# Pair 0's setup, query loads and phi moved in the opening of an attention kernel followed by two MLP layers, with weight decoding from step 6 and the first layer item in any step

## The chip, the cores and the metric

One core of a Trainium2 chip runs the whole kernel. The metric is device time in microseconds (us) of one execution; the kernel before took 1056.87 us (median of 3 runs, 1056.28 to 1060.51).

## What is computed

The reference is causal attention with a memory branch, and two dense layers behind it. B, H, S, D are 4, 8, 576, 64.

```
scores = (q @ k^T) / 8, causal mask;  a = softmax(scores);  local = a @ v
phi(x) = where(x > 0, x, exp(x) - 1) + 1
mem    = (phi(q) @ M_prev) / (phi(q) . z_prev + 1e-6)
x      = g * mem + (1 - g) * local          g = sigmoid(beta), one per head
h = x @ w_in;  x = (h - tanh(h)) @ w_out            # layer 1, 2304 x 512 x 2048
h = x @ w2_in; x = (P(h) / Q(h)) @ w2_out           # layer 2, a cubic over a quadratic
```

## The kernel before

Attention works on pairs of heads: 16 pairs, 0 to 15. A pair has five units, four blocks of 128 query rows and one with the 64 last rows of both heads. The loop runs over steps `s`: unit `u` has its scores in step `u`, so pair `n` begins in step `5n`. In one step the stages follow a fixed list, `ORDER`, and each stage works on an older unit (`LAGS`): scores of the newest unit (TensorE, line 414) with the eviction from PSUM, mask and row minimum (VectorE, line 423); `numer`, the exponentials (ScalarE, line 436) and reciprocal sums (VectorE, lines 441 and 444) one step later; `scale` (GpSimd, line 450) two steps later; `transposes` (TensorE, ScalarE copies) three; `values`, the products `pv` and `pw`, four; `leave`, the copy into `x` (VectorE, line 787), five.

The memory branch needs phi of the queries for each pair. `prep` lists its pieces with the step, relative to the pair's first, in which each is issued: `phi1` (a minimum on VectorE, line 347), `phi2` (an exponential on ScalarE, line 351), `phi3` (VectorE, line 355), `norm1` (GpSimd, line 361, result `pz`), `norm2` (VectorE, from line 370), `norm3` (GpSimd, line 378), and the TensorE transposes `php` (line 388). `late` alters these steps for pair 0. Before the first step `start` issues the key loads, `setup` (the query loads, mask, identity, constants), pair 0's other loads, `setup2` (the gate g and 1 - g, called gg and omg, lines 832 to 839) and pair 0's `phi1`.

All loads go through SyncE's queue (SP). Every engine takes its instructions in program order, so an instruction that waits holds up those behind it on its engine.

Two streams run beside attention. `Background` (`bg`) loads the weights of layer 1, which come as 64-bit words, and decodes them: per half chunk an absolute value (ScalarE, line 164), a clamp, a pair of shifts and two merges (VectorE, lines 166 to 174, tile `wf`), and for the first four chunks a rounding copy (ScalarE) and a remainder (GpSimd, line 186). From step `BG_FROM` on `tick` advances it each step, and starts a half chunk in steps with `s % 5` in `START_A`, (2, 4); from step 34 on only at 2. The other stream is layer 1 itself: when four pairs have left, `fill` calls `advance`. It first prepares the inputs of a tile (`xs`: a rounding copy on ScalarE, a remainder on GpSimd, line 595), and then starts *items*: an item is a *head*, 12 matmuls `h` (line 603), and three steps later a *tail*, 12 matmuls `y` (line 650). Items start in steps with `s % 5` in `ITEM_AT`, (2, 4), the first at step 27. An item waits until its weight chunk is decoded.

Of the kernel before, what the change touches and what calls it, by code (L numbers as in the profile page):

```python
# [18 lines left out]
P = 128  # L19
# [5 lines left out]
ITEM_AT = (2, 4)  # L25
START_A, START_B, MIX_FROM = (2, 4), (2,), 34

BG_FROM = 10
AGE_A, AGE_B, AGE_C = 1, 3, 4

LESS_AT = 4
# [29 lines left out]
def kernel(  # L61
# [21 lines left out]
    nc = tc.nc  # L83
    B, NP, _, _, S = qd.shape
    H, D = 2 * NP, mz.shape[2] // 2
# [4 lines left out]
    TAIL = S - NQ * P  # L90
    TB = NQ * P
# [120 lines left out]
    class Background:  # L212
# [36 lines left out]
        def tick(self, start=True):  # L249
            self.now += 1  # L250
            for item in list(self.live):
                item[0] += 1
                self.held -= item[0] == item[1]
                if next(item[3], self) is self:
                    self.live.remove(item)
            if (
                start and self.ns < self.nl
                and self.now >= self.loaded[self.ns] + self.q[self.ns][4]
                and len(self.live) < len(self.ring["wf"])
            ):  # L260
                _, done, key, work, _ = self.q[self.ns]
                self.ns += 1
                next(work)
                self.live.append([1, done, key, work])
            while self.nl < len(self.q) and self.held < len(self.ring["wraw"]):
                load, _, key, *_ = self.q[self.nl]
                load(*key)
                self.held += 1
                self.loaded.append(self.now)
                self.nl += 1  # L270
# [21 lines left out]
    class Attention:  # L292
# [24 lines left out]
        def load_q(self, n, _=None):  # L317


            n += 1  # L320
            if n < len(self.pair):
                t = self.pair[n]["rq"] = self.cp["rq"][n % 2]
                src = qd[n // NP, n % NP]
                nc.sync.dma_start(t[0:D, P:P + TB], src[0:D, 0, 0:TB])
                nc.sync.dma_start(t[D:P, TAIL:P + TB], src[D:P, 1])
                nc.sync.dma_start(t[0:D, 0:TAIL], src[0:D, 0, TB:S])

        def load_k(self, n, _=None):
# [205 lines left out]

        def late(self, m, f, r):

            if m == 0:
                return r + (f in (self.phi3, self.norm1, self.norm2, self.norm3))
            return r

        def start(self, setup, setup2):

            self.load_k(-1)
            setup()
            self.load_n(0)
            setup2()
            self.phi1(0, None)

        def step(self, s, fill, tick):
            n, i = divmod(s, self.NU)  # L550
            m, at = divmod(s - LAG_T - PHI_AT, self.NU)
            for o in ORDER:
                if o in LAGS:
                    u = self.unit(s - LAGS[o])
                    if u:
                        getattr(self, o)(*u)
                elif o == "fill":
                    fill()
                elif o == "tick":
                    tick()  # L560
                elif o == "phiT":
                    if at == 0 and 0 <= m < len(self.pair):
                        self.phiT(m)
                elif o == "loads":
                    if i == 0 and n < len(self.pair):
                        self.load_n(n + 1)
                        self.load_v(n)
                elif o == "prep":
                    for r, f, arg in self.prep:
                        for m_ in range(len(self.pair)):  # L570
                            if m_ * self.NU + self.late(m_, f, r) == s:
                                f(m_, arg)
# [234 lines left out]
    ]  # L807

    def setup():
        for t in cp["rq"]:  # L810
            nc.vector.memset(t[0:D, TAIL:P], 0.0)
            nc.vector.memset(t[D:P, 0:TAIL], 0.0)
        attn.load_q(-1)
        nc.sync.dma_start(cp["g"], beta.partition_broadcast(P))
        nc.gpsimd.memset(cp["mask"], 0.0)
        nc.gpsimd.affine_select(
            out=cp["mask"][:, TB:TB + P], in_=cp["mask"][:, TB:TB + P],
            compare_op=ALU.is_ge, fill=NEG, base=0, pattern=[[-1, P]],
            channel_multiplier=1,
        )  # L820
        make_identity(nc, cp["ident"])
        for e in range(2):
            r = slice(e * TAIL, (e + 1) * TAIL)
            nc.vector.tensor_copy(cp["mask4"][r], cp["mask"][0:TAIL, TB:TB + TAIL])
        for sm in cp["sm"]:
            nc.vector.memset(sm, 1e-9)
        for pz in cp["pz"]:
            nc.vector.memset(pz[:, :, :, D:D + 1], 1e-6)

    def setup2():  # L830
        g, omg = cp["g"], cp["omg"]
        nc.scalar.activation(g, g, AF.Exp, scale=-1.0)
        nc.vector.tensor_scalar(g, g, 1.0, None, ALU.add)
        nc.vector.reciprocal(g, g)
        nc.vector.tensor_scalar(omg, g, -1.0, 1.0, ALU.mult, ALU.add)
        o2 = omg.rearrange("r (p e) -> r p e", e=2)
        for e in range(2):
            r = slice(e * TAIL, (e + 1) * TAIL)
            nc.vector.tensor_copy(cp["omg4"][r], o2[r, :, e])
# [3 lines left out]
    attn = Attention(x_put, cp, sp, bS, bT, bV)  # L843
    xs_a = Split(x_of, TA, [(wka, f"xs{k}", 1) for k in range(NK)], nc.gpsimd)
    one = Moe1(xs_a, range(NT // TA), TA, FA, wka, bHa, bYa, False, nc.vector)
    flow = {"n": 0, "line": [None, None, None]}

    def advance(start, eager=False):

        line = flow["line"]  # L850
        one.leave()
        if line[0]:
            one.gate1(*line[0])
        if line[1]:
            one.gate2(*line[1])
        if line[2]:
            one.tail(*line[2])
        new = None
        if flow["n"] < len(one.items):
            t, f = one.items[flow["n"]]  # L860
            if (t + 1) * TA <= attn.done * S:
                if t not in xs_a.of and not eager:
                    xs_a.ready(t)
                elif start and (eager or bg.has(1, f)):
                    new = (t, f)
                    one.head(t, f)
                    flow["n"] += 1
                    if eager and f == FA[-1] and (t + 2) * TA <= NT:
                        xs_a.ready(t + 1)
        flow["line"] = [new] + line[:2]  # L870
        return new is not None
# [5 lines left out]
    for f in FB[len(FB) - KEEP:]:  # L877
        bg.add(1, f, w_keep)
    attn.start(setup, setup2)
    mixed = False  # L880

    def fill():
        advance(s % attn.NU in ITEM_AT and s < len(attn.units) - attn.NU)

    for s in range(attn.nsteps):
        if attn.done and not mixed:
# [3 lines left out]
        def tick():  # L890
            if s >= BG_FROM:
                bg.tick(s % attn.NU in (START_A if s < MIX_FROM else START_B))
# [59 lines left out]
    for s in range(ni + 2):  # L952
        if s < ni:
            t, f = items[s]
# [110 lines left out]
```

## Time and profile before

| | |
|---|---|
| profiled execution | 1056.03 us, of which the span from first to last instruction is 1054.2 us |
| runs | median 1056.87 us of 3, 1056.28 to 1060.51 |
| TensorE busy | 1026.5 us (97%) |
| VectorE, ScalarE, GpSimd busy | 785.2, 700.5, 383.5 us |
| granted TensorE clock, mean | 0.996 |

The time of the execution beside its span leaves 1.83 us for what lies outside the first and last instruction. TensorE busy counts matmuls from start to modelled end, so a busy TensorE can still be slower than its peak. In the rows further down PE is TensorE, PEld its weight loads, DVE VectorE, ACT ScalarE, POOL GpSimd, and SPq the issue of a DMA on SyncE's queue.

### The profile page before, as it was taken

What the parts mean: (1) busy time and instruction counts of PE and PEld (TensorE: products, weight loads), DVE (VectorE), ACT (ScalarE), POOL (GpSimd) and SP (SyncE); (2) the same over time, 40 slices, a digit from 0 to 9 for tenths busy, and PEclk for the clock granted to TensorE, in tenths of its full rate; (3) what the DMA queues carried; (4) which work ended last, traced back from release to release, by engine and by line L of the source; (5) the groups of instructions that cost most, each with busy time, mean ns of one, the idle gap of its engine ahead of it and who ended that gap; (6) DMA issues with size and microseconds to landing.
All of it is one profiled execution on the core that took longest, in us unless ns stands there. A gap on an engine that the chain in (4) does not pass through costs nothing.

```text
span 1054.2 us, 18289 instructions
## 1 busy us (share of the span) xinstructions
PE 1026.5 (97%) x6544; PEld 901.8 (86%) x6544; DVE 785.2 (74%) x1737; ACT 700.5 (66%) x1508; POOL 383.5 (36%) x391
## 2 busy tenths in 40 slices
PE   6989999999999999999999998989999999999998
PEld 4657777777699999999999998979999999999997
DVE  5898766766678766767576666998787787877875
ACT  5777775776655543333333456889888888888886
POOL 5788665664534210101010103662332422323221
PEclk9999999999999999999999999999999999999999
DMA  5445343252142334444444331100000000000000
GB/s 154 156 127 164 103 136 110 82 163 82 54 141 80 121 95 136 120 120 122 126 140 123 120 121 61 41 1 30 1 1 31 2 30 1 1 31 1 21 11 30
DMA packets 35147, 84.03 MB, mean 80 GB/s; under 512 B 5872, under 2 KB 7920, under 8 KB 35056
## 3 DMA queue, kind: packets, MB, share of 16 engines
q1 hardware_dynamic: 35056, 82.86, 25.8%
q8 instruction: 51, 0.84, 0.3%
q14 instruction: 40, 0.33, 0.1%
HBM read 66.59 MB, written 16.25 MB: 79 GB/s over the span
## 4 chain that ended last, share of the span: by engine, by line
PE 84%; DVE 9%; ACT 3%; issue 2%; POOL 1%; DMA 1%; SPq 0%; ACTq 0%; POOLq 0%; DVEq 0%
PE h L603 33%; PE y L650 17%; PE y L733 17%; PE s L414 5%; PE tp L466 4%; PE pv L500 4%; PE pw L514 1%; PE pv L488 1%; DVE vA L699 1%; DVE vA L709 1%; PE php L388 1%; DVE gl L639 1%; POOL pz L361 1%; DVE wf L171 1%; DVE vG L711 1%
## 5 line engine op out<-in xcount | busy, mean ns | idle before, releaser
L603 PE MATMUL h<-xs,w 128*128 128x384 f32 (+1 forms) x2448 | 438.2, 327 | 6.2 <-DVE g L715 2.7
L603 PEld LDWEIGHTS h<-xs,w 128*128 128x128 f32 x2448 | 408.5, 188 | 17.0 <-POOL xs L595 3.4
L650 PE MATMUL y<-gh,w 128*128 128x384 f32 (+1 forms) x864 | 216.1, 318 | 0.2 <-ACT gh L638 0.2
L733 PE MATMUL y<-w,gh 128*128 128x512 f32 x576 | 179.7, 393 | 0.0
L650 PEld LDWEIGHTS y<-gh,w 128*128 128x128 f32 x864 | 151.5, 188 | 1.3 <-ACT gh L638 0.6
L450 POOL TENSOR_SCALAR p<-p,sm,omg 128x128 f32<-128x128 f32 (+2 forms) x144 | 116.1, 816 | 74.9 <-ACT p L436 25.2
L650 PE MATMUL y<-gl,w 128*128 128x384 f32 (+1 forms) x432 | 136.9, 317 | 1.2 <-DVE gl L639 0.9
L595 POOL TENSOR_TENSOR xs<-x,xs 128x256 fp32r<-128x256 f32 (+1 forms) x56 | 49.1, 901 | 231.4 <-ACT xs L594 216.1
L632 ACT ACTIVATE g<-h 128x384 f32<-128x384 f32 (+1 forms) x108 | 49.4, 458 | 118.6 <-PE h L603 117.7
L733 PEld LDWEIGHTS y<-w,gh 128*128 128x128 f32 x576 | 107.0, 188 | 17.4
L633 DVE TENSOR_TENSOR g<-h,g 128x384 f32<-128x384 f32 (+1 forms) x108 | 55.0, 509 | 86.2 <-ACT g L632 85.9
L733 PE MATMUL y<-w,gl 128*128 128x512 f32 x288 | 114.1, 396 | 1.1 <-POOL gl L722 1.0
L722 POOL TENSOR_TENSOR gl<-g,gh 128x384 fp32r<-128x384 f32 x48 | 50.6, 1055 | 153.2 <-ACT gh L720 141.4
L470 ACT COPY pT<-tp 128x512 f32<-128x512 f32 (+2 forms) x112 | 55.8, 529 | 60.9 <-PE tp L466 59.1
L722 POOL TENSOR_TENSOR gl<-vG,gh 128x384 fp32r<-128x384 f32 x47 | 51.3, 1092 | 115.1 <-ACT gh L720 112.0
L638 ACT CAST gh<-g 128x384 fp32r<-128x384 f32 (+1 forms) x108 | 51.8, 480 | 58.2 <-PE y L650 55.8
L436 ACT ACTIVATE p<-p,sm 128x128 f32<-128x128 f32 (+2 forms) x144 | 83.8, 591 | 9.3 <-DVE sm L441 4.8
L709 DVE TENSOR_TENSOR vA<-vA,vC 128x384 f32<-128x384 f32 x96 | 57.8, 602 | 41.1 <-ACT vC L703 41.1
L423 DVE CUSTOM_DVE_ANT_0 p<-s,mask 128x512 f32<-128x512 f32 (+4 forms) x160 | 70.3, 476 | 22.2 <-PE s L414 22.0
L414 PE MATMUL s<-rk,rq 64*128 64x128 f32 (+5 forms) x320 | 77.0, 496 | 6.7 <-DMA rq<-in_qd_dram 4.9
L650 PEld LDWEIGHTS y<-gl,w 128*128 128x128 f32 x432 | 81.2, 188 | 2.0 <-DVE gl L639 2.0
L639 DVE TENSOR_TENSOR gl<-g,gh 128x384 fp32r<-128x384 f32 (+1 forms) x108 | 60.7, 562 | 27.7 <-ACT gh L638 27.6
(91 smaller groups left out, 1619.2 us busy)
## 6 DMA issues: line engine op xcount, KB each, us to landing
wraw<-in_w_in_dram SPq DMA_DIRECT2D x32, 512.0 KB, 4.1
wraw<-in_w_out_dram SPq DMA_DIRECT2D x32, 512.0 KB, 4.0
wk<-wf SPq DMA_DIRECT2D x44, 256.0 KB, 4.4
wx<-wk SPq DMA_DIRECT2D x22, 512.0 KB, 3.2
qn<-in_qn_dram SPq DMA_DIRECT2D x16, 320.0 KB, 3.9
vn<-in_vn_dram SPq DMA_DIRECT2D x16, 320.0 KB, 5.3
rk<-in_kd_dram SPq DMA_DIRECT2D x32, 144.0 KB, 5.3
out_dram<-o SPq DMA_DIRECT2D x18, 256.0 KB, 2.0
```

What stands on the lines that cost most here:

```text
L414: nc.tensor.matmul(ps[c][:, 0:k1 - k0], d["rq"][r, c0:c0 + P], d["rk"][r, k0:k1], start=True, stop=True,)
L423: nc.vector.tensor_tensor_reduce(out=pts[-1][:, k0:k1], in0=ps[c][:, 0:k1 - k0], in1=mask, scale=-0.125, scalar=3.0e38, op0=ALU.add, op1=A ...
L436: nc.scalar.activation(pt, pt, AF.Exp, bias=sm[:, 4 + e:5 + e], scale=-1.0, accum_out=sm[:, 2 * e:2 * e + 1],)
L450: nc.gpsimd.tensor_scalar(pt, pt, v["sm"][:, 6 + e:7 + e], og[:, c:c + 1], ALU.mult, ALU.mult)
L470: nc.scalar.copy(t[:, 0:w, :].rearrange("r t c -> r (t c)"), ps[:, 0:w * P])
L603: nc.tensor.matmul(ps[:, 0:T], wi_of(layer, f, wp, k), xs[k][:, xp], start=(n == 0), stop=(n == 3 * NK - 1),)
L633: nc.vector.tensor_tensor(v["g"], v["h"], v["g"], ALU.subtract)
L639: self.lo.tensor_tensor(v["gl"], v["g"], v["gh"].bitcast(F32), ALU.subtract)
L650: nc.tensor.matmul(ps, wo_of(1, f, w)[:, m * P:(m + 1) * P], v[g], start=(first and j == 0 and m % n == 0), stop=(last and j == 2), skip_g ...
L709: nc.vector.tensor_tensor(n["A"], n["A"], n["C"], ALU.mult)
L722: eng.tensor_tensor(o["gl"], o["G"], o["gh"].bitcast(F32), ALU.subtract)
L733: nc.tensor.matmul(acc_of[t][m], g[:, c], wo_of(2, f, w), start=(first and j == 0), stop=(last and j == 2),)
```

## The change

In the opening, two of the three query loads of pair 0 are issued on ScalarE's queue, and ahead of the memsets. `setup2` and pair 0's `phi1` and `phi2` are issued in step 1, behind the scores and exponentials of that step, in place of before step 0 and in step 0. The decoder starts at step 6 in place of step 10. Until the first item has started, an item may start in any step.

```diff
-BG_FROM = 10
+BG_FROM = 6
...
-                nc.sync.dma_start(t[0:D, P:P + TB], src[0:D, 0, 0:TB])
-                nc.sync.dma_start(t[D:P, TAIL:P + TB], src[D:P, 1])
+                eng = nc.sync if n else nc.scalar
+                eng.dma_start(t[0:D, P:P + TB], src[0:D, 0, 0:TB])
+                eng.dma_start(t[D:P, TAIL:P + TB], src[D:P, 1])
                 nc.sync.dma_start(t[0:D, 0:TAIL], src[0:D, 0, TB:S])
...
-            if m == 0:
-                return r + (f in (self.phi3, self.norm1, self.norm2, self.norm3))
+            if m == 0 and f not in (self.load_k, self.load_q):
+                return max(1, r + 1)
             return r
...
             self.load_n(0)
-            setup2()
-            self.phi1(0, None)
+            self.setup2 = setup2
...
                 elif o == "prep":
+                    if s == 1:
+                        self.setup2()
...
     def setup():
+        attn.load_q(-1)
         for t in cp["rq"]:
             nc.vector.memset(t[0:D, TAIL:P], 0.0)
             nc.vector.memset(t[D:P, 0:TAIL], 0.0)
-        attn.load_q(-1)
...
     def fill():
-        advance(s % attn.NU in ITEM_AT and s < len(attn.units) - attn.NU)
+        starts = s % attn.NU in ITEM_AT or not flow["n"]
+        advance(starts and s < len(attn.units) - attn.NU)
```

ScalarE's first instructions before, from the start of the program (`p_0_0` is the exponential of head 0 in unit 0; ISA rows further down are the evictions of line 423):

```order
L832 ACT_TABLE_LOAD
L832 ACTIVATE gg<-gg 128x8
L351 ACTIVATE phi_143<-phi_143 128x640
L436 ACTIVATE p_0_0_155,sm_98<-p_0_0_155,sm_98 128x128
L436 ACTIVATE p_0_1_157,sm_98<-p_0_1_157,sm_98 128x128
L436 ACTIVATE p_1_0_170,sm_99<-p_1_0_170,sm_99 128x256
```

The same place on ScalarE after the change:

```order
L325 DMA rq_102<-in_qd_dram 64x512
L326 DMA rq_102<-in_qd_dram 64x576
L437 ACT_TABLE_LOAD
L437 ACTIVATE p_0_0_147,sm_98<-p_0_0_147,sm_98 128x128
L437 ACTIVATE p_0_1_149,sm_98<-p_0_1_149,sm_98 128x128
L834 ACTIVATE gg<-gg 128x8
L352 ACTIVATE phi_175<-phi_175 128x640
L437 ACTIVATE p_1_0_161,sm_99<-p_1_0_161,sm_99 128x256
```

The gate and phi have moved from ahead of unit 0's exponentials to between those of unit 0 and of unit 1. On VectorE, after the change, the same five small instructions of the gate and the minimum of phi stand behind the evictions of units 0 and 1 and the sums of unit 0:

```order
L424 ISA p_1_1_163,sm_99<-s_1_1_158,mask 128x256
L424 ISA sm_99 128x1
L442 TENSOR_REDUCE sm_98<-sm_98 128x2
L445 RECIPROCAL sm_98<-sm_98 128x2
L835 TENSOR_SCALAR gg<-gg 128x8
L836 RECIPROCAL gg<-gg 128x8
L837 TENSOR_SCALAR omg<-gg 128x8
L841 COPY omg_97<-omg 64x4 x2
L348 TENSOR_SCALAR phi_175<-qn_133 128x640
L424 ISA p_2_0_184,sm_100<-s_2_0_180,mask 128x384
```

Before, the rows from the first `gg` to `phi` stood ahead of the eviction of unit 0; now they stand ahead of that of unit 2. The first decoding rows on VectorE stand, after the change, in pair 1, between the sums of its unit 2 and the copy of pair 0's `pw`:

```order
L445 RECIPROCAL sm_101<-sm_101 128x2
L166 TENSOR_SCALAR wf_0_0_377<-wf_0_0_377 128x512
L167 TENSOR_SCALAR wf_0_0_377<-wf_0_0_377 128x512
L789 COPY x<-pw_399 128x64
L424 ISA p_4_0_422,sm_99<-s_4_0_418,mask 128x512
```

Before, they stood at the same place of pair 2, so the whole series has moved by five steps. On TensorE in pair 5, step 26, after the change (`tp` are transposes, `h_0_0` the first head):

```order
L467 MATMUL tp_3_1_1164<-ident,p_3_1_1014 128x128 x4
L605 MATMUL h_0_0_1170<-xs_0_1106,w_0_500 128x256 x3
L605 MATMUL h_0_0_1170<-xs_1_1109,w_0_500 128x256 x3
L605 MATMUL h_0_0_1170<-xs_2_1112,w_0_500 128x256 x3
L605 MATMUL h_0_0_1170<-xs_3_1115,w_0_500 128x256 x3
L501 MATMUL pv_1064<-pT_2_0_1094,vn_870 64x128
```

Before, `tp_3_1` was followed by `pv` directly, and the first head came one step later. The heads after it follow earlier too, up to step 44: the third input tile may not be prepared before step 44, when eight pairs have left, and takes that step itself. From step 47 on TensorE's order is that of before, so pair 5 has gained one head and one tail, pair 8 has lost a head and pair 9 a tail.

## Rows read from the trace of the kernel before

**Rows 1.** Page, part 4: share of the span in the last chain, by engine.
```profile
PE 84%; DVE 9%; ACT 3%; issue 2%; POOL 1%; DMA 1%; SPq 0%; ACTq 0%; POOLq 0%; DVEq 0%
```

**Rows 2.** Windows, one pair each, pairs 2 to 6: engines' busy time, clock.
```profile
core 0: us, PE busy (x) PEld busy (x) DVE busy (x) ACT busy (x) POOL busy (x), PEclk, DMA share, GB/s
30.87:44.25 13.38, 13.25 (x124) 8.29 (x122) 9.69 (x37) 10.64 (x31) 9.02 (x11) 1.00 0.56 184
44.25:59.76 15.51, 13.36 (x123) 8.32 (x122) 14.45 (x47) 12.65 (x35) 13.86 (x13) 1.00 0.53 156
59.76:76.17 16.41, 14.77 (x123) 8.97 (x122) 15.28 (x54) 11.91 (x33) 13.83 (x13) 0.90 0.48 147
76.17:94.23 18.06, 16.45 (x148) 11.23 (x146) 15.59 (x48) 14.67 (x42) 16.78 (x17) 0.99 0.42 134
94.23:113.06 18.83, 18.83 (x171) 13.96 (x169) 16.88 (x52) 13.06 (x37) 13.36 (x14) 1.00 0.43 128
```

**Rows 3.** The same windows, decoding tile wf alone: DVE, ACT, POOL busy.
```profile
30.87:44.25 13.38, 1.19 (x2) 0.69 (x1) 0.00 (x0) 1.00 0.56 184
44.25:59.76 15.51, 6.23 (x8) 2.81 (x5) 2.72 (x2) 1.00 0.53 156
59.76:76.17 16.41, 6.22 (x8) 2.24 (x4) 2.71 (x2) 0.90 0.48 147
```

**Rows 4.** Timeline of the opening: start, length, instruction, idle before and its releaser.
```profile
0.73 1.28 ACT L832 ACT_TABLE_LOAD   x1 [0.73 <-PEq L1049]
0.74 1.21 SPq L334 DMA_DIRECT2D rk<-in_kd_dram  x2
...
1.99 0.59 SPq L324 DMA_DIRECT2D rq<-in_qd_dram  x1
...
4.90 2.40 PE L414 MATMUL s<-rk,rq 64*128 64x128 f32 x8 [4.90 <-DMA rq<-in_qd_dram]
...
5.66 0.93 PEld L414 LDWEIGHTS s<-rk,rq 64*128 64x128 f32 x6 [0.29 <-issue]
...
7.05 0.21 ACT L832 ACTIVATE gg<-gg 128x8 f32<-128x8 f32 x1 [5.04 <-DMA gg<-in_beta_dram]
7.29 0.17 DVE L833 TENSOR_SCALAR gg<-gg 128x8 f32<-128x8 f32 x1 [4.80 <-ACT gg L832]
...
8.31 0.49 DVE L347 TENSOR_SCALAR phi<-qn 128x640 f32<-128x640 f32 x1
...
8.72 0.28 DVE L423 CUSTOM_DVE_ANT_0 p<-s,mask 128x128 f32<-128x128 f32 x1
8.84 0.74 ACT L351 ACTIVATE phi<-phi 128x640 f32<-128x640 f32 x1 [1.58 <-DVE phi L347]
...
9.48 0.42 DVE L423 CUSTOM_DVE_ANT_0 p<-s,mask 128x256 f32<-128x256 f32 x1
...
10.25 0.49 ACT L436 ACTIVATE p<-p,sm 128x256 f32<-128x256 f32 x1
...
11.14 0.19 ACT L436 ACTIVATION_READ_ACCUMULATOR p<-p,sm 128x1 f32 x1
...
11.71 0.15 DVE L441 TENSOR_REDUCE sm<-sm 128x2 f32<-128x4 f32 x1
```

**Rows 5.** Timeline behind it: GpSimd's scale of unit 1, TensorE's last opening wait.
```profile
12.23 1.52 POOL L450 TENSOR_SCALAR p<-p,sm,omg 128x256 f32<-128x256 f32 x2 [0.42 <-DVE sm L444]
...
19.38 0.33 PE L388 MATMUL php<-ident,phi 128*128 128x128 f32 x1 [0.69 <-ACT pT L470]
```

**Rows 6.** Windows of the opening: busy columns as in rows 2, DMA share and GB/s last.
```profile
3.00:4.00 1.00, 0.00 (x0) 0.00 (x0) 0.00 (x0) 0.00 (x0) 0.00 (x0) 1.00 0.68 224
7.00:8.00 1.00, 0.30 (x1) 0.00 (x0) 0.61 (x4) 0.21 (x1) 0.00 (x0) 1.00 1.03 383
```

**Rows 7.** Timelines of pairs 4 and 5: TensorE's two long waits, then GpSimd's xs.
```profile
71.67 0.95 PE L514 MATMUL pw<-pT,vn 128*64 128x64 f32 x20 [1.58 <-DVE x L787]
...
89.78 0.95 PE L514 MATMUL pw<-pT,vn 128*64 128x64 f32 x20 [0.94 <-DVE x L787]
...
78.76 3.17 POOL L595 TENSOR_TENSOR xs<-x,xs 128x256 fp32r<-128x256 f32 x4
```

## The prediction

> **What bounds the kernel now.** I read the chain that ended last first: 84% of the span is TensorE's own work [rows 1], so a change pays only where TensorE stands still, or runs at half clock. The second view is the windows, cut at each pair's first score. From pair 6 on TensorE is busy for the whole window, 18.83 of 18.83 us [rows 2]: nothing that other engines do there costs anything until they fill that window too. Pair 2 is nearly the same without layer items, 13.25 of 13.38 us. Pairs 3, 4 and 5 are different: 15.51, 16.41 and 18.06 us, with VectorE busy for 14.45, 15.28 and 15.59 of them and, in pair 5, GpSimd for 16.78. There TensorE waits for the others. The reader should see in the next view what separates pair 2 from pairs 3 and 4: the decoder's VectorE work is 1.19 us in pair 2 and 6.23 and 6.22 us in the next two [rows 3]. The last view is the timeline of the opening, where TensorE waits for the queries until 4.90 and is not held up by the opening for good until 19.38 [rows 4, 5].
>
> So three places carry the sum: the opening, the pairs that carry decoding without items, and pair 5, into which an item moves.
>
> **The opening.** Before, the second key half leaves SyncE's queue at about 1.34 (two issues in 1.21 us from 0.74), and the first query load at 1.99, which TensorE sees at 4.90: 2.91 us from issue to use [rows 4]. The second head's first score, which needs both second halves, begins at 5.66; call that moment t. But t does not show up at once: VectorE's first eviction stands behind the gate and phi and starts at 8.72, although TensorE's first eight score matmuls are over at 7.30 [rows 4].
>
> Afterwards ScalarE is free to issue at 0.73, where its table load stands now, so the second query load leaves at about 1.32. With the same 2.91 us, both second halves are there at 4.25: that is the lower bound of t. The upper bound is 5.66, if the transfers only share what they have. The 16 DMA engines are 0.68 busy at 224 GB/s while these loads arrive, and reach 383 GB/s later [rows 6]; there is room, so I take 4.6, nearer the lower bound.
>
> From t the chain now runs through the moved work, since ScalarE's exponentials of unit 1 stand behind phi2, and phi2 waits for VectorE's phi1: 1.64 to the end of unit 1's scores (5.66 to 7.30), 0.42 for the last eviction, 0.52 for unit 0's sum and reciprocal (bounded by unit 1's, 11.71 to 12.23), 1.02 for the gate's five instructions (7.29 to 8.31), 0.53 for phi1 (8.31 to 8.84), 0.74 for phi2, 1.08 for the two exponentials (10.25 to 11.33), and 0.52 to GpSimd's scale of unit 1 [rows 4, 5]. That is 6.47, so the scale starts at 11.07 and not at 12.23. Behind it the order on GpSimd is unchanged, and its work leads on to TensorE's last opening wait at 19.38, so I carry the difference: **-1.2 us**, bounds -1.5 (t = 4.25) and -0.1 (t = 5.66). The 3 us for which VectorE's first eviction is late are not won: gate and phi are only passed on to unit 1.
>
> Some moves cost nothing. ScalarE's two issues, some 0.6 us each, push its 1.28 us table load to an end near 3.2, before any exponential has data; without that cover they would cost 1.2. SyncE has two issues fewer, so beta, the natural queries and pair 1's loads leave 1.2 us earlier; beta is used at 7.05 now and would be there near 5.9, ahead of ScalarE's turn for it. The memsets behind the load have no wait.
>
> **The decoder.** It moves by exactly one pair. Pair 1 takes over the 1.19 us of pair 2, and pair 2 becomes a fully loaded pair like pair 3 [rows 3]. Pairs 3 to 5 stay loaded, since the series continues. What drops out is the last half chunk before attention ends and one after it, both beside TensorE work of layer 1; I cost that at nothing, with 0.5 us either way. A loaded pair without items costs 15.51 - 13.38 = 2.13 by pair 3. By pair 4 it costs 16.41 less what the clock took: at a granted clock of 0.90 that is 0.10 x 16.41 = 1.6 us, so 14.8 - 13.38 = 1.4 [rows 2]. I take the middle, **+1.8 us**. Upper bound: pair 4 as it stands, +3.0. Lower bound: the load hides in TensorE's lead, as the first 1.19 us did in pair 2, and pair 4 keeps its clock, -1.6. Nothing else is gained in exchange: pair 5's first item was not waiting for its weights at step 27. The earlier decoding only lets the fourth item find its chunk at step 32.
>
> **The item.** One head and one tail move from pairs 8 and 9 into pair 5. Pair 6 has two items and pair 2 none, so an item is (18.83 - 13.25) / 2 = 2.8 us of TensorE [rows 2]. Pairs 8 and 9 carry two items each as pair 6 does; I take their windows to be as full, so they give back all 2.8. Pair 5 has 18.06 - 16.45 = 1.61 us in which TensorE stands still, of which 0.94 is the wait for VectorE's copy of `x` before 89.78 [rows 2, 7]. That copy hangs on GpSimd and VectorE, not on TensorE, so the moved head hides in this wait. A new wait: at step 26 TensorE has the head ahead of `pv`, and GpSimd ends the last `xs` at 81.93 [rows 7], about when TensorE gets there; everything behind the head on TensorE would wait with it, some tenths. Gain between 0 (no wait filled) and 1.6 (all); I take **-1.2 us**.
>
> **The sum.** -1.2 + 1.8 - 1.2 = -0.6 us on the profiled execution's 1056.03 us (span 1054.2 and 1.83 around it): 1055.4. The four times at hand are 1056.03, 1056.28, 1056.87 and 1060.51; their middle is 1056.6, 0.5 above the profiled one, so I predict 1055.9. This kernel's runs differ by up to 0.4%, so a change under half a percent, 5.3 us, can hardly be told from none.
>
> **Rivals.**
> *The queries land no sooner.* Four half loads in flight on the same engines might take as long as one behind the other; for it speaks that 0.68 of the engines' time is taken already, against it the later 383 GB/s [rows 6]. The opening then gives 0.1 instead of 1.2: 1057.0. The Trainium skill says this in DMA: Bandwidth & Descriptors, Issuing engines are not separate DMA queues: loads issued by several engines run on the same 16 DMA engines, and only the issue time is saved. By that rule the second query load gains at most its queue's issue time, and the trace of before, with one queue in use, cannot decide it.
>
> *The decoding hides and the clock holds.* Pair 2 enters with TensorE ahead and might absorb the load, as it did with the first 1.19 us, and pair 4 might not lose its clock, which is the lower bound above: -1.6 in place of +1.8, so 1052.5. Against it: VectorE's 14.45 us do not fit into 13.38 [rows 2]. It passes half a percent only if pair 5's waits are filled to the last 0.4 us and the stage behind attention gives its 0.5 too.
>
> *The clock falls more often: slower.* Place: pairs 2 to 5. In pair 4 TensorE waited 1.58 us before 71.67, and the window shows a granted clock of 0.90, so the half clock (1.2 instead of 2.4 GHz) cost 1.6 us [rows 2, 7]. Three pairs instead of two now have such waits without items to fill them. Each further fall costs 1.6: 1057.5 with one, which is already slower than before, and from the fourth on, 1062.3, slower by more than half a percent. The Trainium skill has the rule in TensorE: Matmul & The Clock Gate, Part 1: the slow state is the default and only activity releases the clock. The window of pair 4 agrees with it. Against the rival: pair 3, with a wait of its own, kept a clock of 1.00.
>
> **The numbers.** Likeliest 0.60, range of its own 1054 to 1058; no sooner landing 0.13; hiding and clock 0.13; further falls 0.14. The second rival and the scatter of runs put 0.08 beyond half a percent below, the third 0.05 beyond it above. Faster 0.08, same 0.87, slower 0.05. The range of 8 in 10 is 1052.5 to 1060: it takes in the first two rivals and two further falls of the clock.
>
> **What the profile would show.** The first `s` on TensorE near 4.0 and the second head's near 4.6; VectorE's first eviction near 5.3 and not behind phi; ScalarE's phi between the exponentials of units 0 and 1; GpSimd's scale of unit 1 near 11.1; the last opening wait of TensorE near 18.2. Pair 2's window near 15.5 us with some 6.2 us of `wf` on VectorE; pair 5 near 19.7; pairs 8 and 9 near 17.4 each; pairs 10 on as before. The forecast fails if pair 2 keeps 13.4 us, if pair 5 grows by all of 2.8, if the clock falls in several of pairs 2 to 5, or if the stage behind attention moves by more than 1 us.

## The result, and the profile after

The changed kernel takes 1068.11 us (median of 4, 1067.98 to 1068.98), that of before 1056.57 beside it (4 runs, 1056.25 to 1060.51): ratio 1.0102, 95% interval 1.0078 to 1.0127. It is slower, by some 11 us. The forecast of 1055.9, and its range up to 1060, were wrong. The profiled execution has a span of 1066.3 us, 12.1 more than before, and a mean granted clock of 0.990. The execution of before that was profiled (1056.03) lies at the lower end of that kernel's runs: those beside the experiments have medians from 1057.8 to 1058.0, and against these the change costs some 10 us.

The chain that ended last, by engine, answers to [rows 1]. GpSimd's share has gone from 1% to 3%:

```profile
PE 83%; DVE 9%; POOL 3%; ACT 2%; issue 2%; DMA 0%; ACTq 0%; POOLq 0%; DVEq 0%
```

The windows of pairs 1 to 9, each from a pair's first score to the next one's, answer to [rows 2]:

```profile
core 0: us, PE busy (x) PEld busy (x) DVE busy (x) ACT busy (x) POOL busy (x), PEclk, DMA share, GB/s
14.04:32.66 18.62, 16.47 (x124) 10.07 (x122) 12.08 (x44) 11.33 (x33) 12.25 (x15) 0.82 0.45 150
32.66:48.49 15.83, 13.36 (x123) 8.32 (x122) 14.77 (x47) 12.99 (x35) 13.82 (x13) 1.00 0.54 153
48.49:65.06 16.57, 14.92 (x124) 9.12 (x123) 15.43 (x55) 11.52 (x33) 13.95 (x14) 0.90 0.45 146
65.06:80.18 15.12, 13.43 (x124) 8.31 (x122) 13.72 (x42) 12.61 (x35) 13.57 (x13) 1.00 0.50 160
80.18:101.95 21.77, 19.91 (x170) 14.32 (x170) 17.51 (x58) 15.45 (x44) 18.59 (x18) 1.00 0.37 111
101.95:121.55 19.60, 19.34 (x172) 14.07 (x170) 15.84 (x48) 12.87 (x38) 10.20 (x13) 1.00 0.51 151
121.55:145.08 23.53, 21.77 (x172) 16.27 (x170) 13.44 (x48) 12.61 (x37) 11.81 (x15) 0.85 0.30 92
145.08:162.96 17.88, 17.57 (x159) 12.55 (x157) 11.93 (x42) 11.05 (x34) 9.97 (x11) 1.00 0.38 121
162.96:181.78 18.82, 18.14 (x159) 12.90 (x159) 14.12 (x51) 14.07 (x40) 13.70 (x16) 1.00 0.38 115
```

Pair 1 took 14.94 us before and starts 1.89 earlier now, but lasts 18.62 at a clock of 0.82. Pair 2 grows by 2.45, pair 5 by 3.71. Pair 7, of which the forecast said nothing, took 18.81 us before and 23.53 now, again at a low clock. These are pairs 1 and 7 before:

```profile
15.93:30.87 14.94, 13.44 (x123) 8.24 (x122) 10.77 (x45) 9.68 (x29) 10.75 (x13) 1.00 0.30 84
113.06:131.87 18.81, 18.81 (x172) 13.95 (x170) 12.67 (x43) 13.27 (x40) 12.50 (x15) 1.00 0.37 116
```

From pair 10 on each pair takes 18.8 as before, and the changed kernel stays some 12 us late to its end.

The opening, by the timeline, answers to [rows 4, 5]:

```profile
0.74 0.57 ACTq L325 DMA_DIRECT2D rq<-in_qd_dram  x1
1.34 0.87 ACTq L326 DMA_DIRECT2D rq<-in_qd_dram  x1
...
4.36 0.79 PE L415 MATMUL s<-rk,rq 64*128 64x128 f32 x2 [4.36 <-DMA rq<-in_qd_dram]
5.19 0.29 DVE L424 CUSTOM_DVE_ANT_0 p<-s,mask 128x128 f32<-128x128 f32 x1 [2.70 <-PE s L415]
5.54 4.63 PE L415 MATMUL s<-rk,rq 64*128 64x128 f32 x14 [0.39 <-DMA rq<-in_qd_dram]
...
11.73 1.51 POOL L451 TENSOR_SCALAR p<-p,sm,omg 128x256 f32<-128x256 f32 x2 [2.00 <-DVE sm L445]
...
12.76 0.97 PE L467 MATMUL tp<-ident,p 128*128 128x128 f32 x4 [1.12 <-POOL p L451]
...
15.45 1.19 PE L467 MATMUL tp<-ident,p 128*128 128x128 f32 x6 [0.92 <-POOL p L451]
...
17.54 1.12 PE L389 MATMUL php<-ident,phi 128*128 128x128 f32 x4 [0.90 <-POOL phi L379]
...
18.88 0.47 PE L389 MATMUL php<-ident,phi 128*128 128x128 f32 x1 [0.23 <-ACT pT L471]
```

The first score comes 0.54 us sooner, but the second head's only 0.12 (5.66 to 5.54). While the loads arrive, the DMA share, second to last, is 1.01; it answers to [rows 6]:

```profile
3.00:4.00 1.00, 0.00 (x0) 0.00 (x0) 0.00 (x0) 0.53 (x1) 0.00 (x0) 1.00 1.01 256
```

Between 12 and 18 us TensorE now waits three times, for GpSimd. The windows of that stretch, in steps of 2 us, show it busy for about half the time, and the clock falling at the end of it:

```profile
12.00:14.00 2.00, 1.14 (x8) 0.60 (x8) 1.74 (x7) 1.70 (x6) 2.00 (x3) 1.00 0.28 69
14.00:16.00 2.00, 1.07 (x9) 0.61 (x7) 1.14 (x4) 0.92 (x3) 2.00 (x3) 1.00 0.97 312
16.00:18.00 2.00, 1.01 (x5) 0.78 (x6) 1.93 (x9) 0.40 (x1) 1.35 (x3) 0.78 0.88 263
```

Before, it was busy throughout from 12 to 16, and then:

```profile
14.00:16.00 2.00, 2.00 (x14) 1.14 (x12) 0.95 (x4) 1.41 (x5) 2.00 (x3) 1.00 0.87 289
16.00:18.00 2.00, 1.23 (x11) 0.87 (x10) 1.90 (x9) 0.25 (x1) 1.81 (x2) 1.00 0.78 227
```

By the trace's clock records the half clock (1.2 GHz) lasts from 17.14 to 23.97, just when pair 1's work has come and TensorE hardly pauses: it is busy for 6.21 of these 6.83 us. A second long fall stands at 122.95, 6.83 us again. The timelines of TensorE and GpSimd in pair 5 and at the turn to pair 7 show the other two places:

```profile
84.90 2.33 PE L605 MATMUL h<-xs,w 128*128 128x256 f32 x12
...
91.06 1.67 PE L605 MATMUL h<-xs,w 128*128 128x256 f32 x12 [1.33 <-DVE g L635]
...
117.51 3.18 POOL L597 TENSOR_TENSOR xs<-x,xs 128x256 fp32r<-128x256 f32 x4 [2.74 <-ACT xs L596]
...
121.89 5.05 POOL L451 TENSOR_SCALAR p<-p,sm,omg 128x384 f32<-128x384 f32 x5
...
123.62 0.90 PE L467 MATMUL tp<-ident,p 128*128 128x128 f32 x3 [1.58 <-POOL p L451]
```

In pair 5 the second head waits for the first item's gate. At the turn to pair 7 the next input tile's remainder `xs` stands on GpSimd ahead of a scale for which TensorE waits 1.58 us. Before, that `xs` came in step 35, after this scale; now it comes in step 33, because the fourth item starts in step 32 and not 34.

### The profile page after: what moved, and what is told of

The parts are those of the page before. It is cut to its first block, busy times and chain, and to the rows that moved or that the text cites. A ratio compares the mean times of both kernels' runs of the same rounds, so it can differ in the third digit from the quotient of the medians.

```text
span 1066.3 us, 18293 instructions
## 1 busy us (share of the span) xinstructions
PE 1033.6 (97%) x6544; PEld 906.3 (85%) x6544; DVE 787.2 (74%) x1737; ACT 701.1 (66%) x1508; POOL 386.7 (36%) x391
## 4 chain that ended last, share of the span: by engine, by line
PE 83%; DVE 9%; POOL 3%; ACT 2%; issue 2%; DMA 0%; ACTq 0%; POOLq 0%; DVEq 0%
PE h L605 33%; PE y L652 18%; PE y L735 16%; PE s L415 5%; PE tp L467 4%; PE pv L501 4%; PE pv L489 1%; POOL p L451 1%; POOL xs L597 1%; DVE vA L701 1%; PE pw L515 1%; DVE vA L711 1%; DVE p L424 1%; PE php L389 1%; DVE vG L713 1%
## 5 line engine op out<-in xcount | busy, mean ns | idle before, releaser
L605 PEld LDWEIGHTS h<-xs,w 128*128 128x128 f32 x2448 | 408.5, 188 | 19.7 <-POOL xs L597 4.6
```

What stands on the lines that cost most here:

```text
L605: nc.tensor.matmul(ps[:, 0:T], wi_of(layer, f, wp, k), xs[k][:, xp], start=(n == 0), stop=(n == 3 * NK - 1),)
```

## The experiments

**Theory W**: TensorE's new waits (opening, second head, scale behind `xs`) and the clock falls behind them make the loss, the one behind `xs` only where decoding and item are changed together. **Theory L**: the decoding, a pair earlier, makes all of it, wherever it disturbs. Each run below stands beside runs of the kernel before on the same chip; their medians were 1057.87, 1057.79, 1058.00 and 1057.94 us for runs 1 to 4, 5 to 7, 8 to 11 and 12. Windows have the columns of those above. Runs 1 to 3 and 10 to 12 are made of parts of the change; the others add something to it or to a part. A window or a timeline is one execution's, and the text says where that one lies far from its kernel's median.

**1. The opening alone** (the diff of the change without `BG_FROM` and `fill`).

> The opening's edits alone; decoding from step 10 and first item at step 27 as before. Theory W (TensorE is through its first scores sooner, then waits for GpSimd, and its clock falls as pair 1 begins): pair 1's window is near 18.6 us with a granted clock near 0.8, as in the changed kernel, and the time is 0.5 us less for the chain and 3.4 more for the clock, 1059.5. Theory L (the decoding moved to pair 1 makes pair 1 long): pair 1 stays near 14.9 at clock 1.00, and the time is 1056.1.

1057.43 us, ratio 0.9996 (0.9981 to 1.0011). Pair 1 by the windows:

```profile
14.29:32.57 18.28, 16.27 (x124) 9.80 (x122) 11.34 (x45) 10.64 (x32) 12.10 (x15) 0.81 0.32 96
```

The long pair 1 comes with the opening, without a decoded weight in it, which L had at 14.9. But W's 1059.5 was too high: pair 1 begins 1.64 us sooner than before, where W had 0.5. Pair 4 kept its clock here (15.67, and 16.41 before), and pair 5 took that back (18.85, and 18.06 before).

**2. The decoder alone** (`BG_FROM = 6`).

> Decoding from step 6 alone. Theory W: pair 1 near 14.9 us, pair 2 near 15.7 and nothing else, 1058.4. Theory L: pair 1 near 18 and the pairs behind it late as in the changed kernel, at least 1062.

1061.2 us, ratio 1.0030 (1.0012 to 1.0049). Pairs 2 and 3:

```profile
31.11:46.96 15.85, 13.36 (x124) 8.31 (x122) 14.79 (x47) 13.00 (x35) 13.83 (x13) 1.00 0.51 153
46.96:63.46 16.50, 14.85 (x124) 9.19 (x122) 14.85 (x51) 11.33 (x33) 13.82 (x13) 0.90 0.53 147
```

More than W had (1058.4), less than L (1062 and more with pair 1 near 18; it took 15.21). Pair 2 is as long as in the whole change: +2.47, and this term stands apart from the others.

**3. The item alone** (`starts` in `fill`).

> First item in any step alone. The fourth weight chunk is then not decoded at step 32, the fourth item waits for step 34, and the preparation of the second and third input tile stays at steps 35 and 45. Theory W: pair 5 is longer by 3.7 us (2.8 of work and 0.9 of a wait for the one PSUM bank of the heads), pairs 6 and 7 shorter by 1.4 each, 1057.5. Theory L: the same pairs, but nothing lost, 1055.4.

1060.39 us, ratio 1.0017 (1.0000 to 1.0034). Both theories were too low. The timeline of TensorE in pair 5:

```profile
81.00 1.66 PE L603 MATMUL h<-xs,w 128*128 128x256 f32 x12
...
87.71 2.50 PE L603 MATMUL h<-xs,w 128*128 128x256 f32 x10 [2.55 <-DVE g L633]
```

And the window of the pair:

```profile
76.10:101.42 25.32, 22.28 (x171) 16.16 (x169) 17.98 (x54) 15.88 (x45) 18.48 (x18) 0.85 0.30 95
```

The first head runs without a wait; the second, one step later, waits 2.55 us for VectorE's `g` of the first item. All heads use one PSUM bank, `BANKS_1[3] = [4]`, and `g` frees it. The clock falls at 87.06, during this wait, for 6.83 us. This execution took 1062.51, 2.1 above the median. Not every run has the fall: 6.83 us at half clock alone would bring the mean clock to 0.997, and three of the ten runs have 0.998. These took 1058.52 to 1058.71, and before's three runs at 0.998 on the same chip 1056.17 to 1056.69. So the edit costs about 2.2 us without this fall, and more with it.

**4. The whole change, with `xs` prepared only in a pair's first step.**

```diff
                 if t not in xs_a.of and not eager:
-                    xs_a.ready(t)
+                    if s % attn.NU == 0:
+                        xs_a.ready(t)
```

> The changed kernel with the input tiles prepared only in steps with s % 5 = 0, so at 25, 35 and 45 as before. Theory W (GpSimd's preparation at steps 33 and 44 stands ahead of its scale, for which TensorE waits): pair 7 goes from 23.5 back to about 18.8 with the clock at 1.00, pair 9 to about 18.8 of full work, and the time is 1062. Theory L: the late pairs do not depend on the place of that preparation, 1068.

1062.35 us, ratio 1.0040 (1.0025 to 1.0056): 5.8 us less than the whole change. Pairs 6 and 7, after 19.60 and 23.53:

```profile
101.71:119.56 17.85, 17.54 (x159) 12.53 (x157) 14.17 (x43) 10.79 (x32) 9.14 (x11) 1.00 0.55 165
119.56:137.65 18.09, 17.64 (x158) 12.70 (x158) 13.39 (x51) 14.15 (x40) 13.58 (x16) 1.00 0.41 120
```

W's number, against L's 1068: half of the loss hangs on where `xs` stands. A head less stands in pair 6 and a tail less in pair 7 than before, so both are shorter than before (18.83 and 18.81).

**5. The opening alone, its waits filled.** Transposes of the identity into the tile that the real transposes overwrite afterwards, 10, 8 and 6 of them ahead of units 0, 1 and phi:

```diff
+FILL = {(0, 0): 10, (0, 1): 8, (0, "phi"): 6}
...
                 ps = self.bT(f"tp{n}_{i}_{e0}")
+                idle = FILL.get((n, i), 0) if e0 == 0 else 0
+                for j in range(idle):
+                    nc.tensor.transpose(
+                        ps[:, j % NQ * P:(j % NQ + 1) * P], self.cp["ident"], self.cp["ident"]
+                    )
```

> The opening edits alone (as e1_open, 1057.43, pair 1 18.28 with the clock at half from 16.63 for 6.83 us), and TensorE made to work where it waits for GpSimd in pair 0: 10, 8 and 6 transposes of the identity ahead of the transposes of units 0 and 1 and of phi, into the same PSUM tile, overwritten by the real ones; nothing else waits for them. Theory W (the waits of TensorE let its clock fall as pair 1 begins): no fall near 16.6, pair 1 back to about 15.0, total 1057.4 - 3.3 = about 1054.1. Theory G (pair 1 is long because GpSimd and ScalarE start it late, and the clock falls for something else): pair 1 stays near 18, total 1057 to 1058.

1056.63 us, ratio 0.9987 (0.9977 to 0.9997). The windows of pairs 1 and 5:

```profile
14.62:30.96 16.34, 14.38 (x130) 8.88 (x128) 11.41 (x45) 10.44 (x32) 12.11 (x15) 1.00 0.36 105
75.27:95.52 20.25, 18.05 (x147) 12.69 (x147) 15.72 (x54) 14.28 (x41) 17.16 (x18) 0.92 0.39 119
```

TensorE's timeline has this wait in pair 5:

```profile
83.70 0.66 PE L477 MATMUL tp<-ident,p 128*128 128x128 f32 x4 [1.81 <-POOL p L456]
```

The fall in pair 1 is gone, and 1.94 of its 3.3 us, with work that computes nothing: G is out. What stays is a pair 1 that starts 1.31 us sooner than before and ends where it did (30.96, and 30.87). The total fell by less than expected; in the profiled execution the clock now fell in pair 5 (84.32, 3.41 us), behind a wait of 1.81 us that the run without filling has too, without a fall.

**6. The whole change, pair 7's wait filled** (`FILL = {(6, 2): 14}`).

> The changed kernel (1068.1, pair 7 23.53, clock at half from 122.95 for 6.83 us), with 14 transposes of the identity ahead of the transposes at 123.62, where TensorE waits 1.58 us for the scale that stands behind the input tile's conversion on GpSimd. Theory W: no fall there, pair 7 near 20.2, total about 1064.7. Theory G (the conversion ahead of the scale on GpSimd, 3.18 us, sets pair 7 by itself, whatever the clock): pair 7 stays above 22.5, total 1067 to 1068.

1065.94 us, ratio 1.0078 (1.0063 to 1.0092). The window of pair 7:

```profile
121.72:142.93 21.21, 20.69 (x186) 15.46 (x184) 13.44 (x48) 12.48 (x37) 11.82 (x15) 1.00 0.34 102
```

And the filling in TensorE's timeline, where the wait was:

```profile
122.14 1.75 PE L471 MATMUL tp<-ident 128*128 128x128 f32 x14
```

No fall, and 2.32 us of pair 7 with it; W asked for 3.3, G for none. What stays above 18.81 is 2.40: the 1.75 of filling, which stands where the wait was, a further wait of 0.52 for GpSimd, and 0.13 beside them.

**7. The item alone, but none started in step 27** (`s % attn.NU in ITEM_AT and s != 27`).

> The item edit alone (as e3_item, 1060.39, pair 5 25.32 with a fall at 87.06), but no item started in step 27: the heads stand in steps 26 and 29, not 26 and 27. Theory W (the second head waits 2.55 us for the first item's gate, since all heads share one PSUM bank, and the clock falls behind that wait): pair 5 at most 18.7, no fall in it, total about 1058. Rival X (what costs is the first head one step behind the preparation of its input tile): pair 5 at 21 or more, total at or above 1060.

1058.36 us, ratio 1.0003 (0.9988 to 1.0017). Pairs 5 and 6:

```profile
75.88:95.68 19.80, 17.99 (x160) 12.85 (x158) 17.80 (x52) 15.62 (x43) 18.02 (x18) 0.98 0.40 122
95.68:113.61 17.93, 17.63 (x161) 12.53 (x159) 15.17 (x49) 12.46 (x35) 11.84 (x14) 1.00 0.44 135
```

The total is W's; X's 1060 is out. Pair 5 is 1.1 above W's bound, since the first item's tail now falls into it, and pair 6 is 0.90 shorter than before for the same reason. So most of the item edit's price goes with the second head right behind the first. How much is known only roughly: the medians of runs 3 and 7 differ by 2.0 us, on two chips and with intervals that overlap, and the two windows of pair 5 show more than that, since run 7's profiled execution (1056.48) is 1.9 below its median and run 3's is above.

**8. The opening alone, its waits and pair 5's filled** (`FILL = {(0, 1): 11, (0, 2): 8, (0, "phi"): 6, (4, 4): 16}`).

> The opening edits with filling transposes of the identity as in e5_open_fill, better placed (11 ahead of unit 1's, 8 ahead of unit 2's, 6 ahead of phi's transposes of pair 0), and 16 more ahead of the last transposes of pair 4, where e5_open_fill waited 1.81 us for GpSimd and the clock fell at 84.32 for 3.41 us (pair 5 20.25). Theory W: no fall in pair 1 and none in pair 5; pair 1 at most 16.3, pair 5 about 18.9, total 1056.6 - 1.4 = about 1055.2. Rival S (the fall only shifts to the next wait each time): another fall within pairs 2 to 8, total again 1056.6 or more.

1057.12 us, ratio 0.9987 (0.9977 to 0.9998). Pairs 1 and 5 (pair 2 takes 13.12):

```profile
14.05:30.35 16.30, 15.27 (x138) 9.74 (x136) 11.41 (x45) 10.40 (x32) 12.07 (x15) 1.00 0.38 105
74.65:93.49 18.84, 18.44 (x161) 13.08 (x162) 15.41 (x53) 14.29 (x41) 16.86 (x17) 1.00 0.44 128
```

As W had it, no fall before 656 us, so S is out for this stage; span 1053.6, which is 0.6 less than before's 1054.2. But the runs' median is that of run 5 within their spread (1055.38 to 1058.01), 1.9 above what W gave. Falls of the clock are not the reason: eight of the eleven runs have the profiled one's mean clock, 0.998, and five of these took 1056.90 to 1057.23, the others 1055.38 to 1055.66. What divides them stays unexplained. It is the fastest version found, with run 5, by 0.13%.

**9. The whole change with both fillings** (`{(0, 1): 11, (0, 2): 8, (0, "phi"): 6, (6, 2): 16}`).

> The whole change with both fillings, that of the opening (11, 8 and 6) and that of pair 7 (16). Theory W: no fall near 17 and none near 123, total 1068.1 - 1.8 (opening, as from e1_open to e5_open_fill in pair 1) - 2.2 (as e6_fill7) = about 1064.1. What stands above 1057.6 then is waits and work, not the clock: about 6.5 us. Rival S (the fall shifts to another wait): 1066 or more.

1065.15 us, ratio 1.0066 (1.0047 to 1.0084); span 1061.6. Pairs 2, 5, 6 and 7 (pair 8 takes 17.85):

```profile
30.36:46.20 15.84, 13.36 (x124) 8.32 (x123) 14.78 (x47) 13.01 (x35) 13.81 (x13) 1.00 0.53 153
77.37:99.15 21.78, 19.92 (x170) 14.32 (x170) 17.52 (x58) 15.44 (x44) 18.60 (x18) 1.00 0.40 112
99.15:118.78 19.63, 19.38 (x172) 14.10 (x170) 15.84 (x48) 12.88 (x38) 10.21 (x13) 1.00 0.49 150
118.78:140.02 21.24, 20.81 (x188) 15.70 (x186) 13.44 (x48) 12.50 (x37) 11.82 (x15) 1.00 0.34 102
```

No fall in any pair, as W had it. The median lies between W's 1064.1 and S's 1066, but the profiled span is 4.7 shorter than the whole change's: that much is the clock's, in the profiled executions. By the ratios, 1.0102 and 1.0066, it is 3.8.

**10. Opening and decoder, without the item.**

> The change without its item edit (opening and BG_FROM = 6). The input tile's conversion stays at the steps it has before. If the parts add up: 1057.9 - 0.4 + 3.3 = 1060.8, with pair 7 at 18.9. Rival: opening and decoding disturb each other, 1063 or more, with pairs 2 and 3 longer than e2_decode's 15.85 and 16.50.

1062.52 us, ratio 1.0041 (1.0027 to 1.0055). Pairs 2 and 3 (15.85, 16.48) are those of run 2, so the two do not disturb each other there, and pair 7 takes 18.81. Of the 1.7 us above the sum, 1.36 stand in pair 5 (18.85 in run 1), where the wait of 1.81 us stood again and the clock fell at 89.27:

```profile
80.32:100.53 20.21, 18.00 (x146) 12.62 (x146) 15.72 (x54) 14.31 (x41) 17.17 (x18) 0.92 0.38 120
```

**11. The opening with all queries on SyncE's queue** (`nc.sync` in place of `eng`).

> The opening edits without the change of queue: pair 0's queries issued by SyncE, ahead of the clears of the query tile's zero halves as in the change. If the queue brings nothing (the prediction's rival 'queries land no sooner'): second head's first score at 5.4 to 5.8 (5.54 in the changed kernel), total within 0.7 of e1_open's 1057.43. If ScalarE's queue is what brings the small gain: first score at 4.8 or later, second head's at 6.0 or later, total 1058 or more.

1058.53 us, ratio 1.0013 (1.0001 to 1.0025). The first score is at 4.95, the second head's at 5.53, and GpSimd's scale of unit 1 at 11.73:

```profile
11.73 1.51 POOL L450 TENSOR_SCALAR p<-p,sm,omg 128x256 f32<-128x256 f32 x2 [2.00 <-DVE sm L444]
```

The scale's moment is that of the changed kernel to the hundredth, without ScalarE's queue. So the queue brings the first score forward, but neither the second head's nor the scale. The other executions agree: in the eight with the second queue (the changed kernel, runs 1, 4 to 6 and 8 to 10) the first score is at 4.24 to 4.47 and the second head's at 5.47 to 6.12; in the six without it (before, runs 2, 3, 7, 11 and 12) they are at 4.83 to 5.05 and 5.53 to 5.73. The 0.12 us of the changed kernel is scatter. The totals are undecided: 1.1 us above run 1 on another chip, more than the 0.7 expected, with intervals that overlap.

**12. Decoder and item, without the opening.**

> Decoding from step 6 and the free first item together, the opening as before. If the two only add up: 1057.9 + 3.3 + 2.5 = 1063.7, with pair 7 near 18.9. Theory W (together they bring the fourth item to step 32, so that the next input tile is converted on GpSimd in step 33, ahead of a scale that TensorE waits for): pair 7 at 21 to 23.5 and a total of 1068 to 1070, as long as the whole change, whose opening then brings nothing.

1068.34 us, ratio 1.0100 (1.0079 to 1.0121): as slow as the whole change, 4.6 above the sum of the two. The timelines of GpSimd and TensorE at the turn to pair 7:

```profile
117.32 3.19 POOL L595 TENSOR_TENSOR xs<-x,xs 128x256 fp32r<-128x256 f32 x4 [2.73 <-ACT xs L594]
...
123.43 0.90 PE L466 MATMUL tp<-ident,p 128*128 128x128 f32 x3 [1.58 <-POOL p L450]
```

The same wait, and the same fall (122.73, 6.83 us): pair 7 takes 23.52 at a clock of 0.85. As far as the runs tell, the opening adds nothing to the loss and takes nothing from it. That is a weak statement, since the runs spread from 1065.97 to 1071.71, and in the profiled one the clock fell in pair 1 too, with the old opening (17.50, at a clock of 0.90).

## Why the prediction was wrong

**The account.** In profiled spans the change costs 12.1 us. Run 9 takes 4.7 of it away by keeping the clock. Run 9 and run 8 both have no fall in the pairs; they differ by 8.0, and by the windows: pair 2 +2.72, pair 5 +2.94, pair 6 +0.79, pair 7 +2.43, pair 8 -1.0, together 7.9. Run 8 against before is the opening without its falls, -0.6. 4.7 + 8.0 - 0.6 = 12.1. By the medians, in the forecast's terms: opening -0.4 (forecast -1.2), decoder +3.3 (+1.8), item +2.5 (-1.2), and 4.6 that appear only where decoder and item meet, for which the forecast had nothing. That is 10.0, of the 10 us that the change costs against the same medians of before.

**The opening, -1.2: wrong by two steps.** The step "there is room, so I take 4.6" failed: t was 5.54, and 5.47 to 6.12 over the eight executions with this opening. This is the rival "the queries land no sooner". The 16 DMA engines were 1.01 busy at 256 GB/s between 3 and 4 us, against 0.68 and 224 before [rows 6], so there was no room left, and run 11 reaches the same scale without the second queue. By the Trainium skill (DMA: Bandwidth & Descriptors, Issuing engines are not separate DMA queues) a second issuing engine saves issue time alone; the traces agree: the first load was issued 1.25 us sooner and used 0.54 sooner, and the second was used no sooner, beyond scatter. From t the chain took 6.19 against 6.47 forecast, so the scale came at 11.73, and the last wait at 18.88: a gain of 0.5. The second step, "I carry the difference", failed worse: TensorE had its scores behind it sooner and then waited for GpSimd, and its clock fell into pair 1. With the fall, pair 1 starts 1.89 us earlier and ends 1.79 later. Where the waits are filled and the clock holds, the 0.5 is carried: in runs 8 and 9 pair 1 ends at 30.35, 0.52 earlier than before. Evictions, phi between the exponentials and the first score came as forecast, within 0.4 us.

**The decoder, +1.8: right mechanism, too small.** Pair 2 has 6.55 us of `wf` on VectorE and takes 15.83, near the forecast 15.5; it cost 2.45, inside the bounds. The low one of the two estimates behind the 1.8 was mis-sized: it took 1.6 off pair 4 for the clock, and pair 4 without a fall takes 15.67 (run 1), 0.74 less and not 1.6, so a loaded pair costs 2.3 there too. Run 2 alone costs 3.3 by the medians; its profiled execution has the fall moved from pair 4 to pair 3 (+0.99, -1.08) and pair 5 longer by 0.78.

**The item, -1.2: the step that failed most.** "The moved head hides in this wait" was worked out for one head. Two heads in steps 26 and 27 need the one bank, and the second waits for the gate of the first, 1.33 us in the whole change and 2.55 in run 3. The new wait that the forecast named, at step 26 for `xs`, isn't there in run 3, and in the whole change there is at most a head of 2.33 us in place of 1.66. Pair 5 was forecast at 19.7 and took 21.77. Of the 2.8 that pairs 8 and 9 should give back, pair 8 gave 1.0 and pair 9 nothing (18.82): TensorE's busy time fell by 0.66 there, to 18.14, but new waits took that back. The likely reason is the third tile's `xs`, which GpSimd now begins 0.6 us into that pair (163.57, for 4.06 us) and before 2.6: in run 4, where it stands as before, the pair takes 18.81 with the tail in it.

**What the forecast had no term for: pair 7.** The premise that failed is that from pair 6 on nothing that other engines do costs anything "until they fill that window too". In pair 7 GpSimd is busy for 11.81 of 23.53 us and TensorE has the work of before, but the order on GpSimd makes TensorE wait. The forecast said of the earlier fourth item that it "only" finds its chunk sooner. It is the last of the first input tile's four, and `advance` then prepares the next tile, in step 33 and not 35. On GpSimd it now stands ahead of a scale that TensorE needs. Runs 4 and 12 show its price from both sides: 5.8 us less when `xs` is put back, 4.6 us beyond the sum when decoder and item meet. Of it some 2.2 is the clock's (run 6).

**The rival "the clock falls more often"** had the mechanism and the sign, but not the place or the price. Its place was pairs 2 to 5; the two dear falls stood in pairs 1 and 7, behind waits for GpSimd. Its price of 1.6 each came from one window; 2.3 was measured in pair 7 and about 2 in pair 1. By the Trainium skill (TensorE: Matmul & The Clock Gate, Part 1) the slow state is the default and activity releases the clock; runs 5, 6, 8 and 9 agree, where activity that computes nothing kept it. The falls alone, 4.7 us, would not have passed the half percent.

Right were the pairs from 10 on, and the stage behind attention: 12.2 us late after pair 10, 12.1 at the end.

## What to carry to other kernels

Ahead of moving an item earlier, list everything that its start triggers (here the next tile's preparation) and see on each engine what it then stands in front of; the order of GpSimd showed it before any run. An item's price is not its work alone: two in neighbouring steps that share a PSUM bank wait for each other's reader. And a gain in front of a stretch in which TensorE has no pause is worth carrying only if TensorE comes to that stretch busy. Last, a window is one execution's: see where that execution lies among the kernel's runs before two windows are compared.

## What was not expected of the hardware

- A fall's price depends on what comes next. Before, the fall in pair 4 cost 0.74 (16.41, and 15.67 in run 1), and pair 5 gave 0.79 back (18.06, and 18.85 in run 1), where TensorE else waits 1.81 us for GpSimd.
- The same wait is not always followed by a fall. The 1.81 us in pair 5 stood in runs 1, 2, 5, 10 and 11, and the clock fell in 5 and 10 alone. What decides it stays open. In pair 1 the clock fell in all six profiled executions with the new opening unfilled, in none of the three filled ones, and in one of five with the old opening: run 12, for 3.41 us, where pair 1 took 17.50.
